# Bias and row scale on GpSimd, and a first batch in three chunks, in a hashed attention with an MoE behind it

## The chip, the cores and the metric

The kernel runs on one core of a Trainium2 chip. A core has five engines that run side by side, each with its own queue of instructions in order: TensorE (PE in the profile, with its weight loads as PEld), VectorE (DVE), ScalarE (ACT), GpSimd (POOL) and SyncE (SP, which here only issues DMAs), and 16 DMA engines behind them. The metric is the device time of one execution in microseconds, as a median over runs.

## The reference

Attention over 4 batches, 8 heads, 768 positions and 64 features, in which a query sees only the keys that fall in its hash bucket, followed by a two-layer network (the "MoE") on the 512 features of each position. All is in 32-bit floats.

```python
q_bucket = sum(((q @ proj) > 0) * powers)          # 6 bits, k_bucket alike
scores = where(q_bucket == k_bucket, q @ k.T / 8, -1e9)
attn = exp(scores - max(scores))                   # per row
attn = attn / (sum(attn) + 1e-9)
x = (attn @ v) laid out as [4 * 768, 512]
h = x @ w_in                                       # 512 -> 2048
g = where(h > 0, h, exp(min(h, 0)) - 1)
out = g @ w_out                                    # 2048 -> 512
```

## The kernel before, in words

Precision is kept by splitting: every 32-bit operand becomes a high and a low 16-bit half, and a product is three matmuls (high by high, low by high, high by low). The bucket test is folded into the score matmul: the sign bits are projected on TensorE, made into large numbers (L291) and copied by small DMAs into extra rows of K and Q, so that a key of another bucket gets a large negative score.

The work is cut into *chunks*: a batch has six query tiles of 128 positions a head, and a chunk is a number of them, of all heads, given by `FIRST` for batch 0 (L29) and `OTHER` for the others. Before, each batch is two chunks of three. Heads go in pairs, four pairs a chunk. A *slot* is one query tile of one head: 192 in all, 48 a batch. The main loop (L889) runs over the slots. At slot `G` it issues

- `scores` (L504): four matmuls into a score tile, and the running maximum on VectorE (L520), which writes the scores to SBUF as `pt` and the row's maximum as one column of `m`. Before slot `starts[0]` the odd slots use a second score tile in PSUM; from there on there is one;
- after each second slot, `exps` (L528) for the two: the bias `nb` is the maximum times a scale (L533, 128x2), and then come two exponentials on ScalarE (L536) with row sums into `sm`;
- one slot later, `splits` (L541): the scale of the row, `r`, is made from `sm` (L545, 128x2) and inverted on VectorE (L546); the high half is a product on ScalarE (L143, by the helper `scaled`), the low half one on VectorE (L152, by `rest`), and a transposing DMA from SyncE's queue (L551) brings both to `PT`;
- four slots after a pair's last (`AV_LAG`), `attend` (L553): 36 matmuls of `PT` with the values, and `x`, split again;
- a share of the MoE (`run_moe`), of the preparations that are due (`run_due`) and of the weights (`weights`, six steps a slot).

The MoE of a chunk may begin `MOE_LAGS` = 6 slots after the chunk's last slot (`starts`, L799): at slot 30 for the first chunk before. Its work is spread evenly over the slots up to the next chunk's start. For each of 16 groups of 128 hidden features, `first` (L578) does 12 matmuls (L585) as wide as the chunk (128 columns a query tile), and then exponential, relu and high half on ScalarE (L596, L599, L143) and two instructions on VectorE (L600, L152); `second` (L607) does three matmuls of 512 columns (L621) for each query tile. The results go to HBM by 24 DMAs on GpSimd's queue (L635); beside them and some fills, GpSimd does nothing.

Weights arrive as 64-bit floats, 32 slices, and are decoded in the loop (`wdecode`, L460): one instruction on ScalarE, three on VectorE, and a matmul (L472) that gathers their magnitude. A scale is known only when all 16 slices of a matrix are decoded; after it each slice is split (`wsplit`). Loads of later slices wait for K preparations of later pairs (`w_turn`, L435), and slices whose place in the weights' buffer still serves as staging for the first pairs wait until those are done (`guards`). The preparation of a pair of batch 0 is due a fixed number of slots before its first slot (`PREP0`): 12 for the sums, the scale and the split, 6 for the projection. For Q it is made for each chunk and pair: a load, a sum of squares, powers, two split halves, two transposing DMAs, six projection matmuls and two small copies.

Instructions are written in the order of the loop. A planner then orders those of each engine by priority and by times that it works out for them itself, and puts in the waits. From slot `starts[0]` on (L890), TensorE's order is the written one.

Of the kernel before, what the change touches and what calls it, by code (L numbers as in the profile page):

```python
# [12 lines left out]
AF = mybir.ActivationFunctionType  # L13
ALU = mybir.AluOpType
# [7 lines left out]
P_TOP = 14  # L22
# [3 lines left out]

FIRST = [3, 3]  # L29
OTHER = (3, 3)  # L30
MOE_LAGS = (6, 6, 6)
AV_LAG = 4
# [34 lines left out]
def lsh_attention_moe(  # L67
# [10 lines left out]
    nc = tc.nc  # L78
# [5 lines left out]
    NC = S // P  # L84
    NP = H // 2
    HALF = S // 2
    HC = NC // 2
# [51 lines left out]
    def scaled(kind, o, x, s):  # L139

        e = engine(kind)
        if e == "A":
            nc.scalar.activation(o, x, AF.Copy, scale=s)  # L143
        elif e == "V":
            nc.vector.tensor_scalar(o, x, s, None, ALU.mult)
        else:
            nc.gpsimd.tensor_scalar(o, x, s, 1.0, ALU.mult, ALU.mult)

    def rest(kind, o, x, s, hi):

        if engine(kind) == "V":
            nc.vector.scalar_tensor_tensor(o, x, s, hi, ALU.mult, ALU.subtract)  # L152
        else:
            nc.gpsimd.tensor_scalar(x, x, s, 1.0, ALU.mult, ALU.mult)
            nc.gpsimd.tensor_tensor(o, x, hi, ALU.subtract)
# [90 lines left out]
    def spare(a, b, dt=F32):  # L246

        n = a * b // (2 if dt == F16 else 1)
        free[0] -= n
        return Wf[:, free[0] : free[0] + n].bitcast(dt).rearrange("p (a b) -> p a b", b=b)  # L250
# [15 lines left out]
    for i in reversed(range(STAGES)):  # L266
        end = free[0]
        if i > 0:
            stages[i] = Stage(lambda a, b, dt, name: spare(a, b, dt), FIRST[0])
            stages[i].kf, stages[i].qf = spare(2 * NC, D), spare(2 * FIRST[0], D)  # L270
        guards.append((free[0], end, set(range(i, NP, STAGES))))
# [256 lines left out]
    def exps(st, duo):  # L528

        m, pts = duo[0], duo[1:]  # L530
        w = len(pts)
        nb = small.tile([P, 2], F32, tag="nb", name="nb")
        nc.scalar.activation(nb[:, :w], m[:, :w], AF.Copy, scale=st["sg"][:, 1:2])  # L533
        sm = small.tile([P, 2], F32, tag="sm", name="sm")
        for n, pt in enumerate(pts):
            nc.scalar.activation(  # L536
                pt, pt, AF.Exp, bias=nb[:, n : n + 1], scale=st["sg"][:, 0:1], accum_out=sm[:, n : n + 1]
            )
        return sm, pts

    def splits(sm, pts, PTs):  # L541

        w = len(pts)
        r = small.tile([P, 2], F32, tag="r", name="r")
        nc.scalar.activation(r[:, :w], sm[:, :w], AF.Copy, scale=2.0**-P_TOP, bias=1e-9 * 2.0**-P_TOP)  # L545
        nc.vector.reciprocal(r[:, :w], r[:, :w])  # L546
        for n, pt in enumerate(pts):
            hl = pp.tile([P, 2, S], F16, tag="p", name="hl")
            scaled("p_hi", hl[:, 0, :], pt, r[:, n : n + 1])
            rest("p_lo", hl[:, 1, :], pt, r[:, n : n + 1], hl[:, 0, :])  # L550
            nc.sync.dma_start_transpose(PTs[n].rearrange("p x c e -> p (x c) e"), hl.rearrange("p x e -> p (x e)"))  # L551
# [123 lines left out]
    for b in range(B):  # L675
        c0 = 0
        for n in FIRST if b == 0 else OTHER:
            chunks.append({"b": b, "c0": c0, "nc": n, "xs": [None] * NP})
            c0 += n
        assert c0 == NC and n == HC  # L680
    slots, begin, pairs = [], [], []
    for ci, c in enumerate(chunks):
        for p in range(NP):
# [51 lines left out]
    for ns in groups:  # L735
# [3 lines left out]
        for n in ns:  # L739
            at = begin[n] - (PREP0 if early else PREP)[2]  # L740

            w = 2 * chunks[pairs[n][0]]["nc"]
# [142 lines left out]
    def run_splits():  # L885
        if behind:
            splits(*behind.pop())

    for G in range(starts[-2] + 1):  # L889
        if G == starts[0]:  # L890
            ordered.enter_context(tc.manual_schedule(engines={mybir.EngineType.PE}))
        if G < len(slots):
            n, at = slots[G]
# [61 lines left out]
```

## Time and profile before

| | |
|---|---|
| median of 3 runs | 952.47 us (951.82 to 953.67) |
| profiled execution | 948.24 us, span 946.5 us |
| mean clock of TensorE | 0.94 of full speed |
| TensorE busy | 818.4 us, 86% |
| ScalarE busy | 739.3 us, 78% |
| VectorE busy | 704.0 us, 74% |
| GpSimd busy | 15.7 us, 2% |
| hardware DMA queue | 68.9% of 16 engines |

Lines of the groups read: line, engine, operation, output from inputs, shapes, count, then busy us and mean ns of one, then the engine's idle time just before these and what ended it. Lines of a timeline read: start, duration, engine, line, operation, and in brackets the idle time before it. Durations of successive instructions overlap somewhat, so what an instruction holds its engine for is read from start to start.

### The profile page before, as it was taken

Reading aid. Unit: us, or ns where it says so; the run is one execution under the profiler, and the core shown is the slowest. Engines: PE = TensorE matmul, PEld = TensorE weight load, DVE = VectorE, ACT = ScalarE, POOL = GpSimd, SP = SyncE. Lnnn points to the kernel's source line nnn. Section 1 sums busy time; section 2 is a strip of 40 time slices with the busy share of each in tenths; the row PEclk is TensorE's granted clock in tenths of the full one; section 3 lists DMA queues with packets and bytes.
Section 4 is the critical chain, followed back from the end, with each engine's and each line's share of the span. In section 5 each row is a group of like instructions: output and inputs, shape, how many; then the busy total and the mean of one; then the engine's idle time right before and its main releaser. Section 6 shows DMA issues by size and latency. Waiting matters only on the chain.

```text
span 946.5 us, 14531 instructions
## 1 busy us (share of the span) xinstructions
PE 818.4 (86%) x4975; PEld 420.4 (44%) x4975; DVE 704.0 (74%) x1528; ACT 739.3 (78%) x1469; POOL 15.7 (2%) x49
## 2 busy tenths in 40 slices
PE   2536555888999999988998999998999999999996
PEld 0113222444545555444544455544545555555553
DVE  6899899898867877678777687787878687674332
ACT  4677777999879888789779788889888788885442
POOL 1000000000000000000000000000000000000000
PEclk9956666998999999999999999999999999999998
DMA  9999886776887767696886767795777667556000
GB/s 280 280 207 224 226 231 161 136 141 145 153 167 169 153 113 126 132 187 117 163 180 137 139 109 150 148 181 101 144 155 136 118 119 151 102 101 100 34 1 35
DMA packets 404586, 138.47 MB, mean 146 GB/s; under 512 B 380960, under 2 KB 398880, under 8 KB 404512
## 3 DMA queue, kind: packets, MB, share of 16 engines
q1 hardware_dynamic: 402432, 131.25, 68.9%
q0 software_dynamic: 1920, 6.29, 1.9%
q8 instruction: 39, 0.64, 0.3%
q14 instruction: 35, 0.29, 0.1%
q10 hardware_dynamic: 160, 0.00, 0.0%
HBM read 35.65 MB, written 6.29 MB: 44 GB/s over the span
## 4 chain that ended last, share of the span: by engine, by line
issue 50%; DVE 14%; PE 14%; DMA 13%; ACT 6%; SPq 1%; POOL 1%; POOLq 0%; ACTq 0%; DVEq 0%
PE o L621 4%; PE av L559 4%; PE h L585 3%; DVE pt L520 3%; DMA PT<-hl 3%; DVE hl L152 3%; PE s L508 2%; DMA K<-natk 2%; DMA O<-nat1q 2%; ACT pt L536 2%; DMA W<-in_moe_w_in_dram 1%; DMA U<-in_moe_w_out_dram 1%; DVE W L469 1%; POOL out_dram L635 1%; DVE W L479 1%
## 5 line engine op out<-in xcount | busy, mean ns | idle before, releaser
L621 PE MATMUL o<-W,U 128*128 128x512 f16 x1152 | 280.2, 380 | 3.2 <-ACT W L143 3.1
L585 PE MATMUL h<-x,W 128*128 128x384 f16 x1536 | 279.8, 326 | 0.0
L585 PEld LDWEIGHTS <-W 128*128 128x128 f16 x1536 | 147.5, 98 | 111.1 <-issue 9.9
L536 ACT ACTIVATE pt<-pt,nb,sg 128x768 f32<-128x768 f32 x192 | 195.3, 1019 | 1.7
L152 DVE SCALAR_TENSOR_TENSOR hl<-pt,r,hl 128x768 f16<-128x768 f32 x192 | 189.4, 1011 | 7.5 <-ACT hl L143 7.2
L520 DVE TENSOR_SCALAR_CACHE_REDUCE pt<-s 128x768 f32<-128x768 f32 x177 | 168.0, 949 | 22.9 <-PE s L508 21.9
L143 ACT ACTIVATE hl<-pt,r 128x768 f16<-128x768 f32 x192 | 168.7, 927 | 20.2 <-DVE r L546 19.4
L508 PE MATMUL s<-K,O 128*128 128x384 f16 x708 | 153.3, 340 | 32.2 <-DVE pt L520 26.9
L621 PEld LDWEIGHTS <-U 128*128 128x128 f16 x1152 | 111.0, 98 | 122.7 <-issue 8.9
L559 PE MATMUL av<-PT,vhl 128*64 128x384 f16 x1152 | 115.6, 350 | 27.3 <-DMA PT<-hl 20.8
L600 DVE SCALAR_TENSOR_TENSOR U<-U 128x384 f32<-128x384 f32 x128 | 70.9, 554 | 85.8 <-ACT U L599 84.8
L508 PEld LDWEIGHTS <-O 76*128 76x128 f16 (+1 forms) x768 | 74.7, 102 | 134.7 <-issue 51.2
L596 ACT ACTIVATE U<-h,ch 128x384 f32<-128x384 f32 x128 | 72.9, 570 | 63.7 <-PE h L585 63.6
L152 DVE SCALAR_TENSOR_TENSOR U<-U,sgg 128x384 f16<-128x384 f32 x128 | 78.4, 612 | 53.3 <-ACT U L143 53.3
L559 PEld LDWEIGHTS <-vhl 128*64 128x64 f16 x1152 | 72.8, 117 | 81.7 <-ACT hl L143 17.7
L143 ACT ACTIVATE U<-U,sgg 128x384 f16<-128x384 f32 x128 | 77.8, 608 | 20.5 <-DVE U L600 20.4
L599 ACT ACTIVATE U<-h,ch 128x384 f32<-128x384 f32 x128 | 72.9, 570 | 0.0
L472 PE MATMUL acc<-W,ones 128*128 128x512 bf16 x32 | 16.9, 546 | 35.7 <-DVE W L469 35.5
L536 ACT ACTIVATION_READ_ACCUMULATOR pt<-pt,nb,sg 128x1 f32 x192 | 36.4, 190 | 0.0
L533 ACT ACTIVATE nb<-m,sg 128x2 f32<-128x2 f32 x96 | 27.7, 289 | 6.8 <-DVE pt L520 6.4
L291 DVE TENSOR_SCALAR zb<-z,pjt 64x384 f16<-64x384 f32 (+1 forms) x48 | 29.1, 606 | 3.9 <-PE z L286 3.9
L207 ACT ACTIVATE nat1q<-qst 128x384 bf16<-128x384 f32 x30 | 15.5, 516 | 18.1 <-DMA O<-nat1q 16.0
(103 smaller groups left out, 527.2 us busy)
## 6 DMA issues: line engine op xcount, KB each, us to landing
U<-in_moe_w_in_dram SPq DMA_DIRECT2D x12, 512.0 KB
vf<-in_v_dram SPq DMA_DIRECT2D x16, 384.0 KB
U<-in_moe_w_out_dram SPq DMA_DIRECT2D x12, 512.0 KB
out_dram<-W POOLq DMA_DIRECT2D x24, 256.0 KB, 4.0
qst<-in_q_dram SPq DMA_DIRECT2D x30, 192.0 KB
kst<-in_k_dram SPq DMA_DIRECT2D x14, 384.0 KB
PT<-hl SPq DMA_TRANSPOSE x192
W<-in_moe_w_in_dram SPq DMA_DIRECT2D x4, 512.0 KB
```

Source lines behind the costliest of these rows:

```text
L143: nc.scalar.activation(o, x, AF.Copy, scale=s)
L152: nc.vector.scalar_tensor_tensor(o, x, s, hi, ALU.mult, ALU.subtract)
L291: nc.vector.tensor_scalar(zb[used], t[used], pj["thr"][used, which : which + 1], (MBIT, -MBIT)[which], ALU.is_gt, ALU.mult)
L508: nc.tensor.matmul(s_tile[:, n, :HALF], st[o][:rows, at, :], kst[kk][:rows, j * NC + n * HC : j * NC + (n + 1) * HC, :].rearrange("p a b - ...
L520: top = nc.vector.tensor_scalar(pt.rearrange("p (n e) -> p n e", n=2), s_tile[:, :, :HALF], CLAMP, None, ALU.max, ALU.max, accum_out=duo[0 ...
L536: nc.scalar.activation(pt, pt, AF.Exp, bias=nb[:, n : n + 1], scale=st["sg"][:, 0:1], accum_out=sm[:, n : n + 1])
L559: nc.tensor.matmul(av[j * D : (j + 1) * D], vt[:, j, c, vx, :], PTs[j][:, :, px, c, :], start=n == 0, stop=n == last,)
L585: nc.tensor.matmul(h, WH[:, g * KT + t, wx, fc * P : (fc + 1) * P], c["xs"][t][:, xx, :], start=n == 0, stop=n == 3 * KT - 1,)
L596: nc.scalar.activation(e, h, AF.Exp, scale=c["ch"])
L599: nc.scalar.activation(hp, h, AF.Relu, scale=c["ch"])
L600: nc.vector.scalar_tensor_tensor(e, e, -1.0, hp, ALU.add, ALU.min)
L621: nc.tensor.matmul(o[t][:, :DO], g16[:, gx, t * P : (t + 1) * P], WH[:, NSI + 1 + f, wx, :], start=f == 0 and i == 0, stop=f == NF - 1 and ...
```

## The change

Two things. The bias `nb` and the row's scale before its inversion are made by GpSimd instead of ScalarE, by one instruction each with the same operands (the second one adds first and multiplies then). And batch 0 is three chunks of two query tiles a head in place of two of three; so the first chunk has 16 slots, its pairs begin at slots 0, 4, 8 and 12, the first MoE may begin at slot 22, and the MoE and value matmuls of batch 0 are 256 columns wide. A condition that the last chunk of a batch has three tiles is dropped. The staging of the first pairs shrinks with `FIRST[0]`.

```diff
-FIRST = [3, 3]
+FIRST = [2, 2, 2]
 OTHER = (3, 3)
...
         nb = small.tile([P, 2], F32, tag="nb", name="nb")
-        nc.scalar.activation(nb[:, :w], m[:, :w], AF.Copy, scale=st["sg"][:, 1:2])
+        nc.gpsimd.tensor_scalar(nb[:, :w], m[:, :w], st["sg"][:, 1:2], 1.0, ALU.mult, ALU.mult)
...
         r = small.tile([P, 2], F32, tag="r", name="r")
-        nc.scalar.activation(r[:, :w], sm[:, :w], AF.Copy, scale=2.0**-P_TOP, bias=1e-9 * 2.0**-P_TOP)
+        nc.gpsimd.tensor_scalar(r[:, :w], sm[:, :w], 1e-9, 2.0**-P_TOP, ALU.add, ALU.mult)
         nc.vector.reciprocal(r[:, :w], r[:, :w])
...
-        assert c0 == NC and n == HC
+        assert c0 == NC
```

## The prediction

> **What bounds the kernel now.** I read the page's slices first, then five stages of busy time, then the groups by line and shape, the waits of the longest stage, and single instructions around one pair of slots. A "slot" is one query tile of one head: one score tile and its maximum (L520).
>
> ```profile
> span 946.5 us, 14531 instructions
> PE   2536555888999999988998999998999999999996
> DVE  6899899898867877678777687787878687674332
> DMA  9999886776887767696886767795777667556000
> ```
>
> TensorE is about half busy for the first seven slices (24 us each) and nearly full after them. VectorE and the DMA engines are the full ones early. By stage, all engines (from and to, length, then PE, PEld, DVE, ACT, POOL busy, each with its count, the clock, DMA share, GB/s):
>
> ```profile
> 0.00:165.00 165.00, 83.64 (x373) 33.91 (x373) 145.54 (x355) 115.52 (x222) 2.58 (x25) 0.71 0.90 230
> 165.00:274.00 109.00, 97.22 (x605) 50.53 (x604) 92.35 (x203) 97.11 (x194) 0.00 (x0) 0.95 0.74 145
> 274.00:370.00 96.00, 93.41 (x602) 49.80 (x602) 72.12 (x152) 83.61 (x172) 1.76 (x3) 1.00 0.74 144
> 370.00:855.00 485.00, 460.64 (x2937) 242.51 (x2936) 365.53 (x774) 403.12 (x810) 8.12 (x15) 1.00 0.74 139
> ```
>
> The same stages for the maxima L520 on VectorE alone, where a slot counts two (the maximum and its accumulator read):
>
> ```profile
> 0.00:165.00 165.00, 26.96 (x58) 0.71 0.90 230
> 165.00:274.00 109.00, 22.96 (x48) 0.95 0.74 145
> 274.00:370.00 96.00, 22.00 (x46) 1.00 0.74 144
> 370.00:855.00 485.00, 110.17 (x230) 1.00 0.74 139
> ```
>
> Up to 165 us 29 slots pass, with VectorE 88% and DMA 90% busy and TensorE half idle: this is the weights' decoding, the first K and Q and attention, without a matmul of the MoE. Then 24 slots take 109 us (TensorE and ScalarE both 89%), 23 slots 96 us (TensorE 97%), 115 slots 485 us (TensorE 95%, ScalarE 83%, VectorE 75%), 4.2 us a slot. After 855 us the last chunk's MoE runs alone. So TensorE sets the time from 274 us on; before 165 us VectorE with the DMA does; in between ScalarE is level with TensorE.
>
> The boundary is at the MoE's first matmuls:
>
> ```profile
> 161.60 0.61 PE L472 MATMUL acc<-W,ones 128*128 128x512 bf16 x1
> 165.32 2.76 PE L585 MATMUL h<-x,W 128*128 128x384 f16 x16
> 175.77 2.11 PE L621 MATMUL o<-W,U 128*128 128x512 f16 x9
> ```
>
> The last weight slice is decoded and summed at 161.6 us, and the loop reaches slot 30, where the MoE is let in, at 165.3 us. Two conditions end together: 30 slots, and all weights.
>
> **The change, part by part.** *First batch in three chunks.* The chunk's end moves from slot 24 to 16, and with the lag of 6 the MoE is let in at slot 22 instead of 30. Eight slots fewer precede it. What a slot costs the early stage, and the small operations of the other part:
>
> ```profile
> L152 DVE SCALAR_TENSOR_TENSOR hl<-pt,r,hl 128x768 f16<-128x768 f32 x192 | 189.4, 1011 | 7.5 <-ACT hl L143 7.2
> L143 ACT ACTIVATE hl<-pt,r 128x768 f16<-128x768 f32 x192 | 168.7, 927 | 20.2 <-DVE r L546 19.4 <-DVE ve L191 0.2
> L520 DVE TENSOR_SCALAR_CACHE_REDUCE pt<-s 128x768 f32<-128x768 f32 x177 | 168.0, 949 | 22.9 <-PE s L508 21.9 <-DMA PT<-hl 0.7
> L152 DVE SCALAR_TENSOR_TENSOR U<-U,sgg 128x384 f16<-128x384 f32 x128 | 78.4, 612 | 53.3 <-ACT U L143 53.3
> L143 ACT ACTIVATE U<-U,sgg 128x384 f16<-128x384 f32 x128 | 77.8, 608 | 20.5 <-DVE U L600 20.4
> L599 ACT ACTIVATE U<-h,ch 128x384 f32<-128x384 f32 x128 | 72.9, 570 | 0.0
> L600 DVE SCALAR_TENSOR_TENSOR U<-U 128x384 f32<-128x384 f32 x128 | 70.9, 554 | 85.8 <-ACT U L599 84.8
> L533 ACT ACTIVATE nb<-m,sg 128x2 f32<-128x2 f32 x96 | 27.7, 289 | 6.8 <-DVE pt L520 6.4
> L545 ACT ACTIVATE r<-sm 128x2 f32<-128x2 f32 x96 | 18.5, 193 | 0.3
> L585 PEld LDWEIGHTS <-W 128*128 128x128 f16 x1536 | 147.5, 98 | 111.1 <-issue 9.9
> L257 POOL MEMSET W<- 128x384 f16 x2 | 0.8, 420 | 0.0
> L236 POOL MEMSET pjt<- 32x1 f32 x8 | 0.5, 92 | 0.2
> ```
>
> A slot takes VectorE about 0.95 + 1.01 = 2.0 us; eight take 16 us, and at VectorE's 88% that is 18 us of time. By the early pace (165/29 = 5.7 us a slot) it would be 46 us, which the weights don't allow; if the weights alone pace the stage, it is about 4 us (165.3 - 161.6). The pair preparations of K stand 4, 8 and 12 slots into the loop instead of 6, 12 and 18, and the later weight loads are released by them, so the weights come sooner as well, in a stage whose DMA is already 90% busy. I take -20 us, ends -4 and -46: near the VectorE price, since VectorE's work is what fills the stage, a little more for the weights released sooner.
>
> The eight slots are not saved; they come later, when TensorE is full:
>
> ```profile
> 601.14 3.45 PE L559 MATMUL av<-PT,vhl 128*64 128x384 f16 x36
> 604.52 0.82 PE L508 MATMUL s<-K,O 128*128 128x384 f16 x4
> 605.18 1.46 PE L621 MATMUL o<-W,U 128*128 128x512 f16 x6
> 606.48 1.46 PE L585 MATMUL h<-x,W 128*128 128x384 f16 x8
> 607.78 0.81 PE L508 MATMUL s<-K,O 128*128 128x384 f16 x4
> ```
>
> From start to start, four score matmuls take 0.66 us and the 36 value matmuls of a pair 3.38 us, a sixth of which is 0.56 us. With projections some 1.3 us a slot, so eight cost 10.7 us, at 95% 11 us: +11.
>
> Narrower tiles. An h matmul of 384 columns takes 1.30/8 = 0.163 us, an o matmul of 512 columns 1.30/6 = 0.217 us: both 0.42 ns a column, so 256 columns should take 0.107 us, which still covers a weight load (PEld, 0.098 us by the group). The 16 x 12 x 3 = 576 h matmuls of batch 0 then cost what 384 wide ones did. The value matmuls (432 in place of 288) lose at most 144 x 3.38/36 = 13.5 us if a narrow one is as long as a wide one, and the h matmuls at most 192 x 0.163 = 31 us by the same token. The column price is the nearer row: I take +3, ends 0 and +44. The o matmuls stay as they are.
>
> ScalarE and VectorE pay per instruction. On ScalarE a column costs (927-608)/384 = 0.83 ns, on VectorE (1011-612)/384 = 1.04 ns. An MoE group costs ScalarE 570+570+608 = 1.75 us and VectorE 1.17 us; at 256 columns 1.43 and 0.90 us. Batch 0 has 48 groups instead of 32: ScalarE 68.6 against 56.0 us, VectorE 43.2 against 37.4, with the Q preparations of four more pair-chunks some +15 and +10 us, spread over slots 22 to 78. ScalarE stood at 89% and 87% there, so this isn't free: +4, ends 0 (hidden behind TensorE) and +15. Also, eight slots with two thirds of the MoE's density follow (slots 54 to 78: two tiles in place of three), where TensorE is relieved but the others are not; it is in that +4.
>
> The DMAs keep their bytes: the 12 Q preparations of batch 0 instead of 8 issue 4 loads, 8 transposes and 8 small bit copies more on SP's queue, in stages where DMA is 74% busy. I cost them at nothing; bare, the issues would be 20 x about 1 us of SP.
>
> *Bias and scale on GpSimd.* 96 times two small ScalarE instructions go, 27.7 + 18.5 = 46 us of busy time. From start to start they hold ScalarE for less:
>
> ```profile
> 602.68 0.29 ACT L533 ACTIVATE nb<-m,sg 128x2 f32<-128x2 f32 x1
> 602.87 0.61 ACT L143 ACTIVATE U<-U,sgg 128x384 f16<-128x384 f32 x1
> 605.53 0.20 ACT L545 ACTIVATE r<-sm 128x2 f32<-128x2 f32 x1
> 605.64 0.47 ACT L568 ACTIVATE x<-av 128x384 f16<-128x384 f32 x1
> 606.01 1.75 ACT L143 ACTIVATE hl<-pt,r 128x768 f16<-128x768 f32 x2
> 605.77 0.17 DVE L546 RECIPROCAL r<-r 128x2 f32<-128x2 f32 x1 [1.29 <-ACT r L545]
> ```
>
> 0.19 + 0.11 = 0.30 us a pair of slots, 29 us in all, most of it where ScalarE isn't the bound. What TensorE could get back of it is small:
>
> ```profile
> PE s L508 <- DVE pt L520: 26.9, 28, 3.5
> PE av L559 <- DMA PT<-hl: 20.8, 11, 6.1
> ```
>
> Scores wait for the maximum of the slot before (one score buffer), and VectorE comes to that maximum late where it stood waiting for ScalarE. 48 us of TensorE's waits lie on this chain; I take -6, ends 0 and -29 (all of ScalarE's relief).
>
> Against it stand two more crossings between engines on the chain maximum, bias, two exponentials, sum, scale, reciprocal, split, transpose. The trace shows no such GpSimd operation. Below: the 32x1 memset, 0.09 us; above: the 128x384 memset, 0.42 us, to which a wait can come. Less than the ScalarE operation's 0.19 to 0.29 us is possible too. I take 0.3 us. Behind a late bias stand the two exponentials and all that ScalarE has queued after them; behind a late scale the reciprocal and the maxima behind it on VectorE, then the scores. ScalarE had 0.37 us of other work (L568) between scale and split here, and VectorE has 120 us idle in the long stage: these hide it mostly. 96 x 0.3 us x about a tenth = +3, ends -3 and +28 (each in full). The 24 output DMAs are on GpSimd's queue and wait for their copies; a bias queued behind one waits too, some 24 times. That is in the upper end.
>
> The shared port is the point where a page speaks against this. VectorE's split L152 reads two SBUF tensors for 1.01 us. The Trainium skill, "SBUF — State Buffer", section "Who interferes with whom", says that such an instruction and a GpSimd one that reads SBUF block each other entirely, whichever starts second. No run here shows it yet; its time is a rival's, below.
>
> **The sum**: -20 + 11 + 3 + 4 - 6 + 3 = -5 us on the profiled execution's 948.24 us (span 946.5 and 1.7 around it), 943 us. The median of the runs is 952.47, 4.2 us above the profiled one; so 947.5 us is forecast for the median.
>
> **Rivals.**
>
> (1) *The weights keep the start.* Slots come sooner but the last weight doesn't: start -4, not -20. For it: 161.6 and 165.3 us lie together, and DMA is 90% busy. Against it: fewer transposes and fewer splits stand in the weights' way. -4 + 11 + 3 + 4 - 3 = +11: 963 us; with half the shift 957.
>
> (2) *The hop blocks.* A GpSimd read starts while VectorE is in a two-input instruction (L152 hl and U, L600: 339 us of 946, 36%) and waits up to 1.01 us, 2 us where two follow each other; the reciprocal, in order on VectorE, waits for it, then the next maximum and the scores. At 0.5 us for each of 96 pairs with half of it reaching TensorE: +24 in place of +3, so +16: 968 us. It decides once a hop is longer than the 0.37 us of cover. For it: VectorE already stood 1.29 us for the scale at 604.5. Against it: VectorE is idle a quarter of the time. This is the skill's rule at work; if the port doesn't block, the rival falls.
>
> (3) *ScalarE was the limit* of more than its busy share says, as its 89% between 165 and 274 us suggests: -22 in place of -6, 932 us.
>
> (4) *The parts cancel*: the earlier start is paid back by narrow chunks, and the small operations were hidden anyway: within 2 us of 952.5.
>
> **How the numbers follow.** Forecast 40%, (1) 20%, (2) 12%, (3) 13%, (4) 15%. About 0.2% (1.9 us) is what a measurement of this kernel can tell from no change. Faster: 37 of the forecast's 40 and (3), 50%; same: (4) and 2 of the forecast, 17%; slower: (1), (2) and 1, 33%. The likeliest case's own range is 941 to 951; the range 934 to 964 takes in most of (3) and (1) and leaves out (2) and the far end of (3).
>
> **What would show it.** The first L585 matmul at 140 to 150 us instead of 165.3 (if at 160, rival 1), with 22 slots before it and the last L472 ahead of it. L585 at 256 columns near 0.107 us from start to start. ScalarE's busy time down by some 46 and up by some 15 us; L533 and L545 on POOL at 0.1 to 0.5 us. If the exponentials or the reciprocal wait for POOL for more than 30 us in total and TensorE's wait for L520 grows beyond 27 us, rival 2 holds. If TensorE's share between 370 and 855 us rises to 98%, rival 3. A first L585 before 150 us with no gain at the end would refute the payback of 11 + 7 us.

## The result, and the profile after

The changed kernel takes 963.27 us (median of 4 runs, 960.38 to 967.47) against 953.07 us before: a ratio of 1.0107, with a 95% interval of 1.006 to 1.0155. It is slower, by 10 us. The profiled execution took 967.47 us, with a span of 965.7 us. The forecast was 947.5 us and faster; the measured time lies inside the range of 934 to 964 us, on the wrong side of no change.

TensorE's slices on the page of the kernel after:

```profile
PE   2355556999889689899989999999999999999996
```

TensorE reaches nines at the eighth slice instead of the eleventh, and then falls back: from slice 11 to 17 there are a six and four eights where the kernel before had only nines.

In the prediction's four stages, counted by the maxima L520, 24, 24, 20 and 119 slots pass, where the kernel before had 29, 24, 23 and 115. The early stage loses 5 slots, the third stage 3 with TensorE at 84% instead of 97%, and the long stage wins 4 back.

A cut by time mixes what the slots do, so from here on the stages are cut at slots. The start of slot n is that of the n-th maximum. Slot 30 starts at 167.8 us before and at 192.8 after, slot 54 at 280.5 and 308.8, slot 78 at 376.8 and 405.9, the last slot (191) at 855.0 and 874.3; from there to the end both take 91.4 us. Busy time in these stages (from and to, length, then PE, PEld, DVE, ACT, POOL busy with counts, clock, DMA share, GB/s), before:

```profile
0.00:167.80 167.80, 86.44 (x390) 35.60 (x391) 147.66 (x360) 117.30 (x225) 2.58 (x25) 0.72 0.90 230
167.80:280.50 112.70, 100.92 (x623) 52.28 (x622) 94.49 (x206) 99.47 (x199) 0.00 (x0) 0.95 0.74 146
280.50:376.80 96.30, 93.71 (x604) 49.94 (x603) 72.86 (x153) 83.87 (x173) 1.76 (x3) 1.00 0.74 144
376.80:855.00 478.20, 453.84 (x2900) 238.92 (x2899) 360.53 (x763) 398.73 (x802) 8.12 (x15) 1.00 0.73 138
```

and after, where the first stage is shown in two parts, cut at slot 22, where the MoE is let in:

```profile
0.00:147.60 147.60, 72.42 (x355) 30.99 (x356) 124.60 (x324) 92.27 (x173) 25.25 (x47) 0.83 0.86 227
147.60:192.80 45.20, 34.51 (x268) 22.23 (x269) 40.14 (x96) 37.03 (x73) 3.48 (x7) 0.92 0.67 119
192.80:308.80 116.00, 103.05 (x789) 64.91 (x787) 90.47 (x214) 93.89 (x190) 10.01 (x26) 0.94 0.75 138
308.80:405.90 97.10, 80.33 (x567) 47.47 (x566) 67.89 (x152) 73.91 (x147) 10.72 (x26) 0.93 0.77 145
405.90:874.30 468.40, 451.87 (x2902) 237.68 (x2901) 367.71 (x765) 379.50 (x691) 59.47 (x127) 1.00 0.75 142
```

The account of the span is then +25.0 us to slot 30, +3.3 from there to slot 54, +0.8 to slot 78, -9.8 to the last slot: +19.3, and the spans differ by 19.2. So two things of opposite sign happened. Something in the first 30 slots costs some 25 us and is not returned, and something in the long stage saves some 10. The two profiled executions lie 19.2 us apart and the medians 10.2, since one is a quick execution of its kernel and the other the slowest of its four; so an item of a few microseconds in this account can belong to the execution.

### The profile page after: what moved, and what is told of

Same layout as the page of the kernel before. It is cut to its first block, busy times and chain, and to the rows that moved or that the text cites. A ratio compares the mean times of both kernels' runs of the same rounds, so it can differ in the third digit from the quotient of the medians.

```text
span 965.7 us, 15613 instructions
## 1 busy us (share of the span) xinstructions
PE 825.2 (85%) x5335; PEld 447.1 (46%) x5335; DVE 719.2 (74%) x1593; ACT 716.2 (74%) x1341; POOL 112.8 (12%) x241
## 5 line engine op out<-in xcount | busy, mean ns | idle before, releaser
L585 PE MATMUL h<-x,W 128*128 128x384 f16 (+1 forms) x1728 | 284.2, 310 | 3.1 <-ACT U L599 1.8
L585 PEld LDWEIGHTS <-W 128*128 128x128 f16 x1728 | 167.5, 98 | 102.9 <-issue 14.0
L520 DVE TENSOR_SCALAR_CACHE_REDUCE pt<-s 128x768 f32<-128x768 f32 x181 | 171.9, 950 | 22.6 <-PE s L508 22.2
L508 PEld LDWEIGHTS <-O 128*128 128x128 f16 (+1 forms) x768 | 74.2, 101 | 140.7 <-issue 63.5
L559 PE MATMUL av<-PT,vhl 128*64 128x384 f16 (+1 forms) x1296 | 114.7, 333 | 24.7 <-DMA PT<-hl 16.7
L533 POOL TENSOR_SCALAR nb<-m,sg 128x2 f32<-128x2 f32 x96 | 70.3, 732 | 487.8 <-DVE pt L520 381.2
L596 ACT ACTIVATE U<-h,ch 128x384 f32<-128x384 f32 (+1 forms) x144 | 76.9, 534 | 67.5 <-PE h L585 67.5
L600 DVE SCALAR_TENSOR_TENSOR U<-U 128x384 f32<-128x384 f32 (+1 forms) x144 | 73.1, 508 | 55.6 <-ACT U L599 55.1
L152 DVE SCALAR_TENSOR_TENSOR U<-U,sgg 128x384 f16<-128x384 f32 (+1 forms) x144 | 81.8, 569 | 27.0 <-ACT U L143 25.5
L143 ACT ACTIVATE U<-U,sgg 128x384 f16<-128x384 f32 (+1 forms) x144 | 82.2, 571 | 23.6 <-DVE U L600 23.6
L599 ACT ACTIVATE U<-h,ch 128x384 f32<-128x384 f32 (+1 forms) x144 | 77.0, 534 | 0.0
L545 POOL TENSOR_SCALAR r<-sm 128x2 f32<-128x2 f32 x96 | 26.6, 277 | 257.9 <-ACT pt L536 257.9
L286 PE MATMUL z<-O,pjz 64*32 64x384 f16 (+3 forms) x216 | 28.0, 336 | 8.4 <-DVE x L569 3.1
```

The source lines that it names most:

```text
L508: nc.tensor.matmul(s_tile[:, n, :HALF], st[o][:rows, at, :], kst[kk][:rows, j * NC + n * HC : j * NC + (n + 1) * HC, :].rearrange("p a b - ...
L520: top = nc.vector.tensor_scalar(pt.rearrange("p (n e) -> p n e", n=2), s_tile[:, :, :HALF], CLAMP, None, ALU.max, ALU.max, accum_out=duo[0 ...
L533: nc.gpsimd.tensor_scalar(nb[:, :w], m[:, :w], st["sg"][:, 1:2], 1.0, ALU.mult, ALU.mult)
L559: nc.tensor.matmul(av[j * D : (j + 1) * D], vt[:, j, c, vx, :], PTs[j][:, :, px, c, :], start=n == 0, stop=n == last,)
L585: nc.tensor.matmul(h, WH[:, g * KT + t, wx, fc * P : (fc + 1) * P], c["xs"][t][:, xx, :], start=n == 0, stop=n == 3 * KT - 1,)
L596: nc.scalar.activation(e, h, AF.Exp, scale=c["ch"])
```

## The experiments

**One part at a time.** The kernel before with only the chunks changed, and with only the two operations moved.

```diff
# chunks alone
-FIRST = [3, 3]
+FIRST = [2, 2, 2]
# GpSimd alone
-        nc.scalar.activation(nb...)      (L533)
+        nc.gpsimd.tensor_scalar(nb...)
-        nc.scalar.activation(r...)       (L545)
+        nc.gpsimd.tensor_scalar(r...)
```

> The three chunks alone, both small operations left on ScalarE. Theory A (the chunks cost it, GpSimd pays some of it back): slower by 15 to 25 us, ratio 1.016 to 1.026, with the same early start (first L585 near 138 us) and the lost slots between 140 and 400 us. Theory B (the GpSimd hops cost it, the chunks were a gain as forecast): faster by 2 to 8 us, ratio 0.992 to 0.998.

> Bias and scale on GpSimd alone, two chunks of three. Theory A: faster by 5 to 12 us, ratio 0.987 to 0.995, by slots that pass faster than one in 4.2 us in the long stage. Theory B: slower by 8 to 16 us, ratio 1.008 to 1.017, with VectorE's waits for the scale above 50 us.

Measured: the chunks alone 967.42 us, 1.0164 [1.0125, 1.0204] of the 952.57 us of the kernel before, measured beside it; GpSimd alone 944.63 us, 0.9925 [0.990, 0.995]. The product of the two ratios is 1.0088, inside the interval of the whole change: the parts add. The chunks lose 15 us and GpSimd wins 8. The chunks' stages, cut at slots 30, 54, 78 and 191:

```profile
0.00:191.90 191.90, 107.20 (x628) 54.59 (x628) 165.43 (x420) 134.73 (x278) 2.37 (x25) 0.85 0.84 200
191.90:300.40 108.50, 99.66 (x789) 63.81 (x790) 88.97 (x211) 94.76 (x210) 1.22 (x2) 0.97 0.81 149
300.40:399.90 99.50, 81.98 (x561) 47.14 (x560) 67.02 (x153) 78.63 (x173) 1.08 (x2) 0.91 0.75 144
399.90:875.90 476.00, 453.04 (x2898) 239.26 (x2897) 361.06 (x766) 398.16 (x803) 7.58 (x14) 1.00 0.74 139
```

Against before: +24.1, -4.2, +3.2, -2.2, together +20.9 us, and the spans differ by 21.1. All of the loss is there at slot 30, sooner than theory A had it. Up to that slot VectorE is 88% busy before and 86% with the chunks, but it has 17.8 us more to do (165.43 against 147.66); TensorE has 20.8 us more. VectorE's groups up to slot 30 with the chunks, those that the kernel before does not have there at all:

```profile
L152 DVE SCALAR_TENSOR_TENSOR W<-W,w1s 128x512 f16<-128x512 f32 x13 | 9.7, 748 | 2.6 <-ACT W L143 2.4
...
L152 DVE SCALAR_TENSOR_TENSOR U<-U,sgg 128x256 f16<-128x256 f32 x8 | 3.8, 478 | 1.3 <-ACT U L143 1.3
L600 DVE SCALAR_TENSOR_TENSOR U<-U 128x256 f32<-128x256 f32 x8 | 3.3, 417 | 0.0
```

Those are the splits of the second weight matrix and the first eight MoE groups, 16.8 us of VectorE; more Q preparations make up the rest. At 86% busy, 17.8 us of work takes 20.7 us, which is most of the 24.1.

This sum holds at slot 30, but the time is lost sooner. Slot 0 starts at 36.7 us before and at 44.4 with the chunks, slot 16 at 97.0 and 114.7, slot 22 at 129.4 and 146.0, and the loop lets the MoE in only there. Up to slot 16, before and with the chunks:

```profile
0.00:97.00 97.00, 44.50 (x184) 16.36 (x184) 81.91 (x232) 64.21 (x128) 2.58 (x25) 0.76 0.97 246
```

```profile
0.00:114.70 114.70, 51.94 (x239) 20.18 (x239) 94.91 (x263) 70.37 (x146) 2.37 (x25) 0.91 0.96 242
```

VectorE has 13.0 us more to do up to that slot. By then it has begun on 25 weight slices instead of 17 and split 5 instead of one. So the decoding is crowded into fewer slots first, and from slot 22 to 30, where the kernel before still decodes, the splits of the second matrix and the MoE take its place. There VectorE is 89% busy (41.06 of 45.9 us), and the longest wait of TensorE is 9.7 us for a weight's split on ScalarE. Another cause lies in the same slots: from slot 22 on there is one score tile instead of two, and TensorE keeps the written order, eight slots sooner than before. No run changes these alone; for a maximum, which is what the second score tile spares it, TensorE waits only 0.9 us between slots 22 and 30.

What does the stage that was relieved of this work do? From slot 54 to 78 two MoE tiles are done instead of three. TensorE has 11.7 us less to do than before, ScalarE 5.2 and VectorE 5.8, and the stage takes 3.2 us longer. No engine is above 82% busy in it. Where TensorE stands is in the trace, with the chunks:

```profile
PE av L559 <- DMA PT<-hl: 13.4, 4, 6.9
```

In four places its value matmuls wait for a transpose, 13.4 us together. In the kernel before, this wait comes to 0.2 us in these slots, and in the kernel after to 13.9.

**Is TensorE's work what paces the slots?** If not, taking it away changes little. The kernel before, with 14 of the 16 feature groups of every MoE left out:

```diff
-            for f in range(NF):
-                if f % FG == 0:
+            for f in (0, NF - 1):
+                if f == 0 or c is chunks[0]:
...
-    cost = [NF * c["nc"] * (3 * KT * P + 3 * DO) for c in chunks]
+    cost = [2 * c["nc"] * (3 * KT * P + 3 * DO) for c in chunks]
```

> Two chunks of three, and 14 of the 16 groups of the MoE are left out of every chunk (the output lacks them), so that TensorE, ScalarE and VectorE have little but attention. Theory A2 (the attention chain paces the slots by itself, at about 4 us): slots after the weights are in (slot 54 to 191) still pass at 3.6 to 4.1 us. Theory E (TensorE paces them): 2.6 to 3.2 us, the larger of ScalarE's and VectorE's work without the MoE.

Measured: 855.68 us, a single run. Of the 93 us that the span is shorter (853.3 us), 57 lie behind the last slot, where the last MoE has nothing beside it. The two windows that hold slot 54 to the last, with all engines and then for L520 alone (two instructions a slot):

```profile
277.00:370.00 93.00, 64.53 (x325) 28.89 (x324) 59.38 (x126) 65.08 (x131) 1.63 (x3) 0.70 0.76 148
370.00:818.00 448.00, 302.19 (x1517) 134.41 (x1515) 295.21 (x630) 311.61 (x606) 6.50 (x12) 0.70 0.77 146
```

```profile
277.00:370.00 93.00, 23.09 (x49) 0.70 0.76 148
370.00:818.00 448.00, 108.15 (x226) 0.70 0.77 146
```

24.5 slots in 93 us are 3.8 us a slot, 113 in 448 us 3.96, against 4.0 and 4.2 with the whole MoE, and no engine is above 70% busy (the DMA engines 77%). So without that work the slots still take about 3.9 us each, and TensorE's 95 to 97% in the kernel before sits just above this pace. What holds the slots there, by the waits between 290 and 800 us (total us, times, longest us):

```profile
PE s L508 <- DVE pt L520: 110.8, 94, 3.5
...
DVE x L569 <- ACT x L568: 63.8, 19, 4.8
...
ACT x L568 <- PE av L559: 59.8, 20, 4.4
...
PE av L559 <- DMA PT<-hl: 45.0, 20, 3.9
```

It reads as a ring: scores wait for the maximum before them, VectorE stands in its order behind a split of `x`, which waits for ScalarE, that for the value matmuls, and those for the transposes. That this ring is the whole of the 3.9 us is argued from the waits, not shown. The clock of TensorE was granted at 0.70 here, against 1.00 before, so the pace at full clock isn't known.

**Can the loss be spread or delayed away?** Four variants of the chunks alone: the later MoE starts spread evenly over the slots (22, 40, 60, 78), the preparations of batch 0 due later, and the start of all MoE put off to slot 30, 46, 62, 78. The last needs two more buffers for `x`, for which a buffer of `pp` (the tiles `pt` and `hl` in SBUF) is given up, and so has a control of its own.

```diff
# all: FIRST = [2, 2, 2], and
# even
-MOE_LAGS = (6, 6, 6)
+MOE_LAGS = (6, 8, 12, 6)
# prep
-PREP0 = (100, 12, 12, 6)
+PREP0 = (100, 8, 8, 4)
# late
-MOE_LAGS = (6, 6, 6)
+MOE_LAGS = (14, 14, 14, 6)
# late, and the control with nothing else
-    pp = ctx.enter_context(tc.tile_pool(name="pp", bufs=8))
+    pp = ctx.enter_context(tc.tile_pool(name="pp", bufs=7))
-        x16 = xp.tile(..., bufs=2 * NP)
+        x16 = xp.tile(..., bufs=2 * NP + 2)
```

> Three chunks, small operations on ScalarE, and the MoE of batch 0 spread evenly: starts at slots 22, 40, 60 and 78 instead of 22, 38, 54 and 78 (lags 6, 8, 12). Theory A2 (the loss is that slots 54 to 78 hold a tile less of MoE and don't pass faster for it): 5 to 12 us faster than the three chunks with even lags, ratio to before 1.004 to 1.011. Theory A3 (narrow chunks cost by themselves, wherever they stand): as before it, 1.013 to 1.020.

> Three chunks, small operations on ScalarE, and the preparations of batch 0's first pairs due 8 and 4 slots ahead instead of 12 and 6, so that they stand as many pairs ahead as before the change. Theory F (the chunks lose their time before slot 30, because preparations of three pairs and the weights crowd in front of the first slots): the first maximum some 5 us sooner than at 44.4 us, slot 30 before 182 us, ratio 1.003 to 1.012. Theory A3 (narrow chunks cost by their width wherever they stand): no change, 1.014 to 1.019.

> Three chunks, small operations on ScalarE, the MoE of batch 0 let in at slots 30, 46 and 62 (lags 14) instead of 22, 38 and 54, so that as much MoE stands ahead of each slot as before the change. Two more x tiles make that possible, one score buffer less (7) makes room; the two controls have these too. Theory H (what is put ahead of slot 30, splits of weights and a tile of MoE, is paid in full, as VectorE is the bound there; what is taken from later slots gives nothing back): slot 30 sooner than in the control with three chunks by 10 us or more, and 0.5 to 1.5% faster than that control. Theory A3 (narrow chunks cost by themselves): within 0.4% of that control.

> Control: the three chunks (small operations on ScalarE, lags of 6) with two more x tiles and 7 score buffers instead of 8. All theories: 1.01 to 1.03 of before.

Measured: even 1.0159 [1.0135, 1.0184], prep 1.0151 [1.0116, 1.0186], both like the chunks alone at 1.0164, so theories A2 and F fail; with the later preparations slot 30 starts at 193.6 us, no sooner. Late 1.0127 [1.0088, 1.0167], and its control 1.0186 [1.0153, 1.022]: the delay by itself wins 0.6%, though the intervals overlap. Slot 30 starts at 184.3 us with it, 7.4 us sooner than in the control and less than the 10 us of theory H. Up to slot 30, late and then control:

```profile
0.00:184.30 184.30, 93.56 (x488) 43.55 (x489) 155.42 (x397) 124.07 (x249) 2.36 (x25) 0.81 0.86 208
```

```profile
0.00:191.70 191.70, 107.42 (x628) 53.69 (x628) 164.00 (x419) 135.57 (x276) 2.36 (x25) 0.87 0.84 200
```

8.6 us of VectorE's work gone from ahead of slot 30 move it by 7.4 us. (The delay also keeps the second score tile until then, so the move isn't VectorE's alone to explain.) The rest stays: 155.42 us is still 7.8 us more than the kernel before, since 9 of the weight splits (6.7 us) and the extra preparations remain ahead of it. And most of the loss stays: 1.0127 against the 1.0017 of two chunks with the same buffers (below), though the MoE starts at the same slot. So what the delay moves is the smaller part of the loss; that the crowded decoding and the remaining splits are the rest is argued from VectorE's sums, not shown by a run.

In slots 54 to 78 the late version has three tiles of MoE again, as before the change: TensorE is busy for 95.23 of 95.5 us, where its control has 81.43 of 99.3. Those 13.8 us of work cost the stage nothing.

**Is the time then independent of TensorE?** The kernel before, with the MoE put off by 12 slots instead of 6, so that the second tile set has only 18 slots (60 to 78) to be done in, and the same buffers without the delay as control.

```diff
-MOE_LAGS = (6, 6, 6)
+MOE_LAGS = (12, 12, 6)
```

> Two chunks of three, the first MoE let in at slot 36 and the second at 60 (lags 12) instead of 30 and 54; tiles and buffers as in the controls. Theory H (slots pace the kernel, the MoE runs in their shadow): within 0.4% of the control with two chunks, or faster. Theory T (the prediction's: TensorE is the bound behind the weights, and MoE work that starts 6 slots later is late at the end): slower by 6 x 1.3 = 8 us or more, 0.8% over that control.

> Control: the kernel before with two more x tiles and 7 score buffers instead of 8. All theories: 1.000 to 1.015 of before.

Measured: 1.0108 [1.0079, 1.0138], and the control 1.0017 [0.9999, 1.0035]. The delay costs 0.9%, as theory T had it and more than theory H allowed. The dense stretch from slot 60 to 78, all engines:

```profile
305.20:392.00 86.80, 86.11 (x541) 45.53 (x540) 60.09 (x128) 67.80 (x136) 1.75 (x3) 1.00 0.68 119
```

Here TensorE is 99% busy, at 4.8 us a slot: it is the bound when a slot carries a sixth of an MoE tile instead of an eighth. So there are two limits, TensorE's work and the slots' own pace, and the kernel before sits near both: with an eighth of a tile a slot, slots 54 to 78 took 96.3 us, with 93.71 of TensorE, and the same slots took 92.6 us (277.3 to 369.9) with most of the MoE left out. That would be why little can come back where work is taken out, while work put into a full stage costs. It doesn't explain all: with the chunks, these slots took 99.5 us at 82% of TensorE, above either limit. TensorE stands there for the transposes, by the 13.4 us above; why these come late no run settles.

**Buffers.** Whether the transposed tiles `PT` (two buffers) make the pace: a third one, which needs the room of two buffers of `pp` and one of `vpool` (the values); a control that gives up the same room for nothing; and, on the mixed version below, one more buffer of `pp` for one of `vpool`.

```diff
# third PT: all three; control: the first two; last: vpool 6 and pp 9
-vpool bufs=7
+vpool bufs=6
-pp bufs=8
+pp bufs=6
-ptp bufs=2
+ptp bufs=3
```

> The kernel before with three buffers for the transposed weights PT instead of two; to make room, 6 value buffers instead of 7 and 6 score buffers instead of 8. Against the next run, which has that alone. Theory G (slots are paced by the PT buffers: the first two transposes of a pair leave only when the value matmuls of the pair before have ended): 1 to 3% faster than the next run, slots 54 to 191 in less than 4.1 us each. Rival (the pace comes from the order of the engines' work around the maxima): within 0.5% of the next run.

> The kernel before with 6 value buffers instead of 7 and 6 score buffers instead of 8, PT as before: the control for the run before it. All theories: slower than before or the same, ratio 1.000 to 1.03.

> The mixed kernel (bias on VectorE, scale on GpSimd, two chunks of three) with 9 score buffers instead of 8 and 6 value buffers instead of 7. If the score buffers hold the slots back (6 of them cost 1.9%, with one value buffer less), 9 give something: ratio 0.975 to 0.985. If 8 are enough: 0.985 to 0.990.

Measured: third `PT` 1.0183 [1.0157, 1.021], control 1.0194 [1.0169, 1.0218]: alike, so that the third buffer is worth nothing that can be told. The mixed version with nine buffers of `pp` and six of `vpool` came to 1.0084 [1.0059, 1.0108], 2% above the same version with eight and seven. The seventh buffer of `vpool` seems to be worth about 2%, though no run takes it away alone.

**Which half of the GpSimd part gains?** The bias alone on GpSimd, the scale alone on GpSimd, both on VectorE instead, the bias on VectorE with the scale on GpSimd, and the bias on VectorE alone; all with two chunks of three.

```diff
# bias alone / scale alone: nc.gpsimd in one of the two places
# both on VectorE
-        nc.scalar.activation(nb...)
+        nc.vector.tensor_scalar(nb...)
-        nc.scalar.activation(r...)
+        nc.vector.tensor_scalar(r...)
# mixed: nc.vector for nb, nc.gpsimd for r;  last: nc.vector for nb, r unchanged
```

> Only the bias on GpSimd, two chunks of three. Theory A: faster, 0.992 to 1.000. Theory B: slower, about 1.005 to 1.01, since the bias is the hop that takes 0.73 us on average in the changed kernel and ScalarE waited 50 us for it.

> Only the scale of the row sums on GpSimd, two chunks of three. Theory A: faster, 0.992 to 1.000. Theory B: slower, about 1.003 to 1.01, since VectorE waited 73 us for it in the changed kernel against 7 us for ScalarE's before.

> Bias and scale on VectorE (the same two instructions), two chunks of three. Theory C (the gain of moving them is that they no longer stand in ScalarE's queue, 1.0 us for each): a gain like GpSimd's or a little less, ratio 0.990 to 0.998, since VectorE pays 0.16 us for each of 192. Theory D (what helped was only ScalarE's relief, and VectorE is as full): no change, 0.998 to 1.003. The port theory makes no statement on this run.

> The bias on VectorE, the scale on GpSimd, two chunks of three. Theory C (what counts is to leave ScalarE's queue by the shorter way: the bias behind its maximum on the same engine, the scale on an engine that is empty): at least the gain of either alone, ratio 0.986 to 0.992. Rival (the gains are the planner's order and don't add): 0.991 to 1.0.

> Only the bias on VectorE, two chunks of three; beside the run with only the bias on GpSimd (1.012) it tells whether GpSimd is the wrong engine for the bias or the bias shouldn't leave ScalarE alone. Theory P (on GpSimd the bias loses against VectorE's two-input instructions, about 1 us each): 0.992 to 1.000. Theory O (the planner's order with only one of the two moved is the bad one): 1.005 to 1.015.

| bias on | scale on | median us | ratio |
|---|---|---|---|
| GpSimd | ScalarE | 963.21 | 1.0124 [1.0095, 1.0154] |
| ScalarE | GpSimd | 944.35 | 0.9921 [0.9897, 0.9944] |
| GpSimd | GpSimd | 944.63 | 0.9925 [0.990, 0.995] |
| VectorE | VectorE | 943.65 | 0.9912 [0.9886, 0.9937] |
| VectorE | GpSimd | 941.23 | 0.987 [0.9846, 0.9894] |
| VectorE | ScalarE | 952.62 | 0.9999 [0.9983, 1.0015] |

The gain is the scale's, and it comes wherever the scale is taken off ScalarE; the bias gains nothing by itself. With the scale on GpSimd, moving the bias to VectorE as well seems to bring another 0.5%: 0.987 against 0.9921, in intervals that just fail to meet. What the scale waited for is seen on ScalarE of the kernel before, one pair:

```profile
451.09 0.21 ACT L536 ACTIVATION_READ_ACCUMULATOR pt<-pt,nb,sg 128x1 f32 x1
453.43 0.49 ACT L568 ACTIVATE x<-av 128x384 f16<-128x384 f32 x1 [2.14 <-PE av L559]
453.82 0.20 ACT L545 ACTIVATE r<-sm 128x2 f32<-128x2 f32 x1
```

The row sum was there at 451.30 us. ScalarE's next instruction in order was the split of `x`, which stood 2.14 us for the value matmuls, and the scale stood behind it until 453.82. With the scale on GpSimd, one pair of the kernel with that alone, ScalarE and then GpSimd:

```profile
603.48 0.19 ACT L536 ACTIVATION_READ_ACCUMULATOR pt<-pt,nb,sg 128x1 f32 x1
603.57 0.60 ACT L143 ACTIVATE U<-U,sgg 128x384 f16<-128x384 f32 x1
```

```profile
603.76 0.18 POOL L545 TENSOR_SCALAR r<-sm 128x2 f32<-128x2 f32 x1 [4.73 <-ACT pt L536]
```

It starts 0.09 us after the sum, though ScalarE has gone on to something else. Averaged over the 56 pairs of slots 78 to 189, worked out from the starts and ends in the traces: the scale starts 1.04 us after the end of the second exponential on ScalarE and 0.18 us on GpSimd, and a pair takes 10.07 us from the end of its second maximum to that of its last split before, 8.69 with the scale on GpSimd, 9.06 in the mixed version. The mixed version is the faster of the two all the same, so a pair's length alone doesn't set the pace. The planner also gives each version an order of its own; how much of a gain is that order's no run separates. The stage from slot 78 to the last takes 478.2 us before, and these, scale alone and mixed:

```profile
387.00:852.20 465.20, 451.44 (x2900) 238.53 (x2899) 367.04 (x763) 393.12 (x745) 20.34 (x72) 1.00 0.75 142
```

```profile
388.70:850.40 461.70, 450.55 (x2899) 239.08 (x2898) 373.00 (x820) 379.17 (x690) 19.80 (x72) 1.00 0.75 143
```

TensorE's work is the same, within 1%, and its share rises from 95% to 97 and 98%. The mixed version beats both kernels: 1.3% under the one before.

The bias alone costs 1.2% on GpSimd and nothing on VectorE, as theory P had it. Why it costs nothing on GpSimd together with the scale stays open. It is slow there, by its group in the version with the bias alone:

```profile
L533 POOL TENSOR_SCALAR nb<-m,sg 128x2 f32<-128x2 f32 x96 | 92.7, 966 | 731.3 <-DVE pt L520 571.3 <-DVE qm L186 73.8 <-ACT hl L143 28.6
```

and 966 ns are more than with both on GpSimd and two chunks (723 ns). In the first of these versions 75 of the 96 biases overlap a two-input instruction of VectorE and take 1.16 us on average, in the second 78 and 0.83 us; the others take 0.27 us in both (counted in the traces). So the waits for VectorE, of the next experiment, are longer here. The difference of 0.24 us a pair is 23 us over 96 pairs if all of it counted, so it could be the loss of 10 us; no run shows that it is.

**What the port costs.** A kernel that computes nothing of the reference: chains of twelve GpSimd operations of the bias's and of the scale's form, alone (`none`), beside a stream of VectorE instructions with two SBUF inputs of 128x768 (`two`), and beside one of maxima from PSUM (`max`).

```diff
+    nc.vector.scalar_tensor_tensor(o, x, m[:, 0:1], hi, ALU.mult, ALU.subtract)      # two, x16
+    nc.gpsimd.tensor_scalar(b, c, sg[:, 1:2], 1.0, ALU.mult, ALU.mult)               # bias, x12
+    nc.gpsimd.tensor_scalar(b, c, 1e-9, 2.0**-14, ALU.add, ALU.mult)                 # scale, x12
```

> The two small GpSimd operations by themselves (the kernel computes nothing else; its output is zeros): 12 of each form, a ScalarE copy between them, first with VectorE idle, then beside a stream of two-input VectorE instructions like L152, then beside a stream of maxima like L520 that read PSUM. Port theory: alone and beside the maxima both forms take 0.2 to 0.3 us, beside the two-input stream 0.5 to 1.3 us. Rival: the bias takes longer than the scale by its form (a column as its scalar) in all three.

Measured, by groups (the kernel takes 84.91 us):

```profile
L100 DVE SCALAR_TENSOR_TENSOR oscale<-x,mtwoscale,hi 128x768 f16<-128x768 f32 x16 | 15.3, 1013 | 0.0
...
L111 POOL TENSOR_SCALAR bias_two<-d,sg 128x2 f32<-128x2 f32 x11 | 6.0, 546 | 3.6 <-ACT d L115 3.6
L113 POOL TENSOR_SCALAR scale_two<-d 128x2 f32<-128x2 f32 x11 | 5.5, 497 | 3.5 <-ACT d L115 3.5
L111 POOL TENSOR_SCALAR bias_max<-d,sg 128x2 f32<-128x2 f32 x11 | 4.8, 437 | 3.6 <-ACT d L115 3.6
L111 POOL TENSOR_SCALAR bias_none<-d,sg 128x2 f32<-128x2 f32 x11 | 2.9, 268 | 3.6 <-ACT d L115 3.6
...
L113 POOL TENSOR_SCALAR scale_none<-d 128x2 f32<-128x2 f32 x11 | 2.1, 193 | 3.5 <-ACT d L115 3.5
L113 POOL TENSOR_SCALAR scale_max<-d 128x2 f32<-128x2 f32 x11 | 2.1, 193 | 3.5 <-ACT d L115 3.5
```

The means of the groups mix two cases, which the single operations tell apart. VectorE's stream of two-input instructions pauses at 27.50 and at 40.53 us, before the chains `two` are over: up to there all but the first operation of each chain take 0.60 to 0.61 us, and the last ones, with VectorE idle, 0.27 (bias) and 0.19 (scale). And some two-input instructions run between the maxima, where they slow the chain `bias_max`, on VectorE and then GpSimd:

```profile
50.97 2.89 DVE L100 SCALAR_TENSOR_TENSOR oscale<-x,mtwoscale,hi 128x768 f16<-128x768 f32 x3
```

```profile
50.49 0.27 POOL L111 TENSOR_SCALAR bias_max<-d,sg 128x2 f32<-128x2 f32 x1 [0.33 <-ACT d L115]
51.09 1.03 POOL L111 TENSOR_SCALAR bias_max<-d,sg 128x2 f32<-128x2 f32 x1 [0.33 <-ACT d L115]
```

Every bias of that chain that overlaps maxima alone takes 0.27 us, as with VectorE idle; those that overlap a two-input instruction take 0.61 to 1.73 us. So the rival falls: the form matters by 75 ns and no more. A delayed operation ends 0.05 to 0.14 us after a two-input instruction of VectorE does, so it waits for the rest of the one that it meets, up to all of it, and for the next where it meets two. In the chains one operation passes for each instruction of VectorE, every 0.94 and 0.93 us. VectorE's own instructions are no longer for it: 1013 ns, as in the kernel before (1011). This is the rule that the prediction named from the Trainium skill, "SBUF — State Buffer", section "Who interferes with whom", and the trace bears it out for GpSimd's side of it, at 0.60 to 0.61 us against 0.27 and 0.19; that VectorE would be held up as well isn't seen.

## Why the prediction went wrong, step by step

**What bounds the kernel: read half right.** "TensorE sets the time from 274 us on" came from its 95 to 97%. It is one of two limits that lie within 2% of each other: in slots 54 to 191 TensorE has 547.6 us of work, and with most of the MoE left out, at a clock of 0.70, they still took 541.3 us, which no busy share showed. Pricing the eight slots that come later by TensorE's time rests on this reading.

**-20 for the earlier start, +11 for the eight slots that come later: this trade failed, by the payback.** The start itself held: the first MoE matmul came even sooner than forecast, on TensorE after:

```profile
137.73 2.12 PE L585 MATMUL h<-x,W 128*128 128x256 f16 x9
...
148.18 0.61 PE L472 MATMUL acc<-W,ones 128*128 128x512 bf16 x2
...
166.81 1.47 PE L585 MATMUL h<-x,W 128*128 128x256 f16 x12
168.12 1.46 PE L621 MATMUL o<-W,U 128*128 128x512 f16 x6
```

at 137.7 us instead of 165.3, a shift of 27.6 us, and of 22.0 with the chunks alone (143.3 us). What failed is the price of what comes behind it. From the first MoE matmul to the end the forecast added 11 + 3 + 4 = 18 us; with the chunks alone these stretches are 781.2 us before and 824.3 us after, 43 us more. The prediction priced a later slot by the 1.3 us that its attention adds on TensorE, as if TensorE set the pace wherever the slots came to lie; slots 22 to 30, the first behind the new start, took 5.7 us each, with TensorE 75% and VectorE 89% busy. And it gave no price to the work that enters the early stage as the MoE comes sooner, above all the splits of the second matrix.

Slot 22 itself, though, by its maximum, starts at 147.6 us after and at 129.4 before: VectorE falls behind before the MoE has well begun, with the weights' decoding crowded into fewer slots. And an earlier start is worth time only if the work that it brings forward fits beside what is there, and if the place that it leaves becomes shorter. Neither held. Ahead of slot 30 VectorE was the bound, as the prediction itself says, and by slot 30 the MoE and the second matrix's splits had brought it 17 us more work (chunks alone). Slots 22 to 30 take 45.2 us after, with TensorE at 76% and VectorE at 89%. In the stage that lost a third of its MoE, slots 54 to 78, TensorE fell to 83% and the stage was 0.8 us longer (3.2 with the chunks alone), with TensorE waiting for transposes. The four terms of the chunks, -20 + 11 + 3 + 4 = -2 by the forecast, measured +15 us (chunks alone). The late-start run shows a part of the first half: with 8.6 us of VectorE's work out of the way, slot 30 comes 7.4 us sooner; the rest of that half is argued from VectorE's sums. The relieved stage shows the second half, in the kernel after and with the chunks alone. The test that the prediction had set itself, a first L585 before 150 us with no gain at the end, came out, and it refutes the payback.

**+3 for narrower tiles: about right.** Twelve narrow h matmuls take 168.12 - 166.81 = 1.31 us from start to start, 0.109 us each, where 0.107 was forecast. TensorE's busy time grew from 818.4 to 825.2 us, 7 us, some of it in stages where it isn't the bound.

**+4 for ScalarE and VectorE: the right doubt, far too small.** It named the eight slots with two thirds of the density and the extra preparations. VectorE's time ahead of slot 30 belonged here, and even the term's upper end of +15 is less than the 17 us that VectorE alone had more to do there.

**-6 and +3 for GpSimd: the sign of the first right, that of the second wrong.** Together -3 forecast, -8 us measured. The scale's crossing to GpSimd was priced as a loss, because the operation's duration was compared and not its place in the queue: 0.28 us against 0.19 us in duration, but 0.18 against 1.04 us of waiting in front of it. The groups after:

```profile
L533 POOL TENSOR_SCALAR nb<-m,sg 128x2 f32<-128x2 f32 x96 | 70.3, 732 | 487.8 <-DVE pt L520 381.2
L545 POOL TENSOR_SCALAR r<-sm 128x2 f32<-128x2 f32 x96 | 26.6, 277 | 257.9 <-ACT pt L536 257.9
```

The scale is within the forecast 0.1 to 0.5 us, the bias is above it. Of the 96 biases, 81 overlap a two-input instruction of VectorE and take 0.82 us on average, the other 15 take 0.26 (counted in the trace). ScalarE's busy time fell by 23 us, where the forecast had 31.

**Rival 1 (the weights keep the start)** gave 963 us, the measured time, by a mechanism that did not happen: the last weight was summed at 148.2 us instead of 161.6 and the MoE began early. That its number came out is luck.

**Rival 2 (the hop blocks).** Its signs appeared, in the waits after:

```profile
DVE r L546 <- POOL r L545: 72.9, 69, 2.6
...
ACT pt L536 <- POOL nb L533: 50.2, 51, 4.7
...
PE s L508 <- DVE pt L520: 29.7, 30, 3.5
```

Both waits are above 30 us and TensorE's is above 27, and yet it is not the cause: GpSimd alone has 67.1, 59.8 and 31.6 us in the same three places and is 0.75% faster. The blocking is real, 0.56 us for a bias that meets it; it doesn't reach the end. That the engines wait longer there because they wait less elsewhere is likely, not shown. The mark that was set for this rival could not tell the two apart.

**Rival 3 (ScalarE was the limit)** is nearer to the GpSimd part than the forecast was, though not by its busy share: it was ScalarE's order that held the chain, not its 83%. Its sign, TensorE at 98% between 370 and 855 us, didn't come: 464.15 of 485 us are 96%.

## What to carry to other kernels

An engine at 95% can sit beside a second limit that no busy share shows, here probably a chain through in-order queues; before counting on time given back where an engine was relieved, take most of its work out of one version and see what pace is left. Price work that starts earlier in the stage that it moves into, by that stage's fullest engine: add up that engine's microseconds there, and not the shift of the start. Put a tiny operation of a chain on an engine whose queue has nothing that waits in front of it; the scale took 0.08 us longer on GpSimd and started 0.86 us sooner, which won.

## What was not expected of the hardware

- A 128x2 operation on GpSimd takes 193 ns with immediate scalars and 268 ns with one scalar from a column, about what ScalarE takes (193 to 289 ns). Beside a stream of VectorE's two-input instructions it takes 0.60 to 0.61 us in a chain, because it waits for the rest of the instruction that it meets; where it met nearly a whole one it took 1.02 us, and where it met two 1.73. VectorE's instructions kept their 1013 ns. Beside maxima that read PSUM it takes no longer than alone.
- In the real kernels the bias took 0.72 to 0.97 us on GpSimd, a mean of two cases: 0.26 to 0.27 us where it met no two-input instruction of VectorE, and 0.82 to 1.16 us where it did, up to 4.42 us.
- TensorE's granted clock was 0.70 in slots 54 to 191 of the kernel with most of the MoE left out, where it is 67 to 69% busy, against 1.00 in the same slots before.
